# Turning the keys before the result, and longer gaps between copies and the products that use them, in a fused recurrence and expert kernel

## The chip, the cores and the metric

The kernel runs on one core of one Trainium2 chip. The metric is the device time of one execution in microseconds (us). The kernel before takes 1080.8 us (median of 4 runs, 1079.32 to 1081.3). All runs in this document are of the state "fast": none took over 1.5% longer than the fastest run of its kernel. A single core has no second die to be compared with, so the only sign of disturbance is the granted clock of TensorE (the share of its full speed at which it was let run, as the trace records it), which was recorded for each run and which matters here.

## The reference

Two blocks follow each other. The first is a gated linear recurrence over 768 positions for 4 batches and 8 heads of width 48. The second mixes 4 experts, each a two-layer network of width 1024, over the 3072 rows that the first block makes.

```python
for t in range(S):                                  # S = 768
    state = alpha[:, :, t, :, None] * state + einsum('bhd,bhe->bhde', k[:, :, t], v[:, :, t])
    y[:, :, t] = einsum('bhd,bhde->bhe', q[:, :, t], state)
x = y.transpose(0, 2, 1, 3).reshape(3072, 384)
p = domain_probs / (domain_probs.sum(-1, keepdims=True) + 1e-09)
for e in range(4):
    out += p[:, e:e + 1] * (relu(x @ w1[e]) @ w2[e])
```

## The kernel before

The recurrence is cut into 24 *units*, one for each chunk of 128 positions and each batch. A unit is a Python generator: every `yield` ends a step, and each step sends some instructions to several engines. The experts run in groups of up to four units (512 rows), and the steps of later units are dealt out between the expert matmuls of earlier ones. The program gives each engine one list of instructions, so a step's place decides how much other work lies between a copy on ScalarE and the product on TensorE that needs it.

The last steps of a unit, cut to what matters:

```python
        copy_q(6)                       # beat 11: ScalarE copies the last queries
        next_q(6)
        yield
        ...                             # beat 12: far = products across a chunk, then sc = levels 4 and 5
        yield
        parts = lat.rearrange("p (r s i) c -> p r s i c", s=2, i=2)
        ...                             # beat 13: ScalarE copies far to lat
        yield
        for s in range(2):              # beat 14: ScalarE copies near to lat
            rows = slice(HALF * s, HALF * (s + 1))
            nc.scalar.copy(out=lat[rows, :, rows], in_=near[rows])
        KT = KTs[-1]
        yield
        yps = ps.tile([P, KC, P], F32, name="yps", tag="w")
        ...                             # beat 15: the result, yps, from lat, v, QT and the state
        yield
        if cb < NCB - 1:
            KB = AT                     # beat 16: keys turned on TensorE, copied by ScalarE
            nc.scalar.copy(out=KB, in_=turned(lambda p: KT[:, p, :]))
            yield
            sps = ps.tile([P, NP, 2, D], F32, name="sps", tag="w")
            ...                         # beat 17: sps = keys x values, added to the state
```

And how steps get their place. `deal` computes for each unit an interval in the scheduler's own count of time, and `advance` sends the steps that have fallen due:

```python
    BEATS = 17
    ...
                events += [(begin + (end - begin) * (j + 1) / BEATS, u, run) for j in range(BEATS)]
    ...
    def advance(spent):
        nonlocal clock
        clock += spent
        while waiting and clock >= waiting[0][0]:
            next(waiting.popleft()[2], None)
```

Units 0 and 1 have their own hand-made order. Units 2 to 5 must be done during the first expert group, which is also when the weights are split into parts (ScalarE and VectorE) and stored for later (`kept`). Their intervals are less than half as long as those of later units.

## Time and profile before

| before, profiled run | value |
|---|---|
| span | 1079.8 us |
| TensorE busy | 1055.5 us (98%) |
| TensorE waits, total idle | 24.3 us |
| of it: yps behind lat, far behind queries | 8.4 us, 4.6 us |
| stretches at half clock before the end | 82.0 to 85.4 and 123.0 to 129.8 us |

The kernel is bound by TensorE, so only idle time and slow time on TensorE count. The view of waits names for each idle stretch what ended it. A window view gives busy time in a stretch together with the granted clock. Its columns are: stretch; length; busy us (instructions) of TensorE, of its weight loads, of VectorE, ScalarE and GpSimd; granted clock; DMA share; GB/s. For the kernel before, in the two stretches behind the long waits and one later on:

```profile
82.00:86.00 4.00, 4.00 (x60) 2.93 (x60) 3.96 (x8) 2.92 (x9) 0.53 (x1) 0.57 0.35 125
122.00:130.00 8.00, 5.64 (x54) 3.73 (x55) 4.33 (x11) 4.66 (x11) 0.53 (x1) 0.57 0.60 237
167.00:171.00 4.00, 4.00 (x45) 2.82 (x40) 3.93 (x9) 1.69 (x4) 1.06 (x2) 1.00 1.01 424
```

The granted clock is 0.57 in the first two: TensorE is nearly at half speed there. The share of busy time doesn't show this, since a slow matmul counts as busy.

### The profile page before, as it was taken

The page shows a single profiled execution, that of the slowest core. Times are in us where ns is not written, and L with a number is a line of the kernel's source. Part 1 is how long each engine was busy: PE and PEld are TensorE (multiplying, and loading weights), DVE is VectorE, ACT ScalarE, POOL GpSimd, SP SyncE. Part 2 cuts the span into 40 slices and gives each one's busy share as a digit, 9 for nine tenths or more (in the row PEclk, how much of TensorE's full clock was granted, in tenths as well). Part 3 has the DMA queues.
Part 4 walks back from the last instruction along what each step waited for, and adds up shares of the span by engine and source line. Part 5 has one row for each costly group of instructions (what it writes and reads, how often), then busy time and mean ns, then how long its engine had stood idle before and what let it go on. Part 6 is the DMA issues. An engine that isn't in the chain of part 4 may idle for free.

```text
span 1079.8 us, 21595 instructions
## 1 busy us (share of the span) xinstructions
PE 1055.5 (98%) x8460; PEld 899.6 (83%) x8460; DVE 774.5 (72%) x1711; ACT 566.8 (52%) x1202; POOL 32.7 (3%) x71
## 2 busy tenths in 40 slices
PE   8889899999999999999999999999999999999998
PEld 8767677676777798898898998888989889898988
DVE  5588678656557878777877786986878866666565
ACT  5786766764747455536446445555564543323232
POOL 2000000000000100000000000000000000000000
PEclk9999899999999999999999999999999999999999
DMA  8597679886686968659568568595594643544440
GB/s 124 155 329 227 213 230 378 301 315 240 234 295 208 399 203 318 253 147 351 204 221 324 195 228 320 159 327 222 168 352 146 249 191 136 215 172 180 182 182 33
DMA packets 158838, 251.67 MB, mean 233 GB/s; under 512 B 120112, under 2 KB 135344, under 8 KB 136208
## 3 DMA queue, kind: packets, MB, share of 16 engines
q1 hardware_dynamic: 149600, 208.82, 56.2%
q0 software_dynamic: 5760, 41.29, 9.7%
q8 instruction: 67, 1.10, 0.4%
q10 hardware_dynamic: 3376, 0.17, 0.3%
q14 instruction: 35, 0.29, 0.1%
HBM read 207.79 MB, written 42.47 MB: 232 GB/s over the span
## 4 chain that ended last, share of the span: by engine, by line
PE 80%; DVE 8%; ACT 6%; issue 2%; SPq 2%; DMA 1%; ACTq 0%; DVEq 0%
PE ops L615 26%; PE one L531 21%; PE two L531 10%; PE ops L619 9%; PE sc L333 5%; PE yps L425 3%; PE tp L265 2%; ACT qb L307 2%; PE one L523 2%; PE sps L454 1%; DVE near L343 1%; DVE hT L571 1%; PE far L388 1%; DVE t L544 1%; SPq L211 1%
## 5 line engine op out<-in xcount | busy, mean ns | idle before, releaser
L615 PE MATMUL ops<-w,hT 128*128 128x384 f32 x1728 | 318.6, 340 | 2.8 <-DVE acc L649 2.8
L615 PEld LDWEIGHTS ops<-w,hT 128*128 128x128 f32 x1728 | 299.1, 188 | 8.2 <-DVE acc L649 4.1
L531 PE MATMUL one<-xT,w 128*128 128x512 f32 x960 | 253.7, 400 | 0.8 <-DMA w<-kept 0.5
L531 PEld LDWEIGHTS one<-xT,w 128*128 128x128 f32 x960 | 175.9, 188 | 42.0 <-issue 2.4
L542 ACT ACTIVATE t<-one 128x512 f32<-128x512 f32 (+1 forms) x192 | 106.5, 555 | 163.8 <-PE one L531 144.1
L307 ACT COPY qb<-QT 64x256 f32<-64x256 f32 x336 | 136.5, 406 | 72.0 <-DVE QT L288 34.8
L569 ACT ACTIVATE hT<-t 128x512 fp32r<-128x512 f32 (+1 forms) x160 | 94.3, 589 | 111.3 <-DVE t L544 110.1
L571 DVE SCALAR_TENSOR_TENSOR hT<-t,hT 128x512 fp32r<-128x512 f32 (+1 forms) x160 | 102.0, 638 | 60.5 <-ACT hT L569 58.8
L531 PE MATMUL two<-xT,w 128*128 128x512 f32 x480 | 136.3, 392 | 0.0
L619 PE MATMUL ops<-hT 128*128 128x384 f32 x384 | 135.8, 497 | 0.0
L544 DVE TENSOR_TENSOR t<-t,two 128x512 f32<-128x512 f32 (+1 forms) x160 | 100.8, 630 | 39.5 <-ACT t L542 21.1
L581 DVE SCALAR_TENSOR_TENSOR hT<-hT 128x256 fp32r<-128x256 f32 x288 | 112.0, 421 | 4.4
L531 PEld LDWEIGHTS two<-xT,w 128*128 128x128 f32 x480 | 90.2, 188 | 19.8
L619 PEld LDWEIGHTS ops<-hT 128*128 128x128 f32 x384 | 70.0, 192 | 40.5 <-issue 1.4
L343 DVE COPY_PREDICATED near<-masks,sc 128x256 f32<-128x256 uint8 x144 | 77.0, 535 | 18.0 <-PE sc L333 14.9
L314 DVE TENSOR_TENSOR QT<-QT,dec 128x256 f32<-128x256 f32 x144 | 60.7, 421 | 34.3 <-ACT qb L307 33.9
L333 PEld LDWEIGHTS sc<-qb,KT 128*64 128x64 f32 x2304 | 73.3, 139 | 9.2 <-issue 7.1
L333 PE MATMUL sc<-qb,KT 128*64 128x64 f32 x2304 | 77.6, 224 | 0.2 <-ACT qb L307 0.2
L649 DVE SCALAR_TENSOR_TENSOR acc<-ops,p_all,acc 128x384 f32<-128x384 f32 x82 | 49.4, 612 | 29.1 <-PE ops L615 14.2
L326 DVE TENSOR_TENSOR KT<-KT,dec 128x256 f32<-128x256 f32 x144 | 60.2, 418 | 2.8 <-PE tp L265 2.8
L325 ACT COPY KT<-KT 128x256 f32<-128x256 f32 x144 | 59.7, 415 | 3.1
L549 DVE TENSOR_TENSOR hT<-t,two 128x512 f32<-128x512 f32 x32 | 22.0, 688 | 35.5 <-ACT t L542 28.6
(88 smaller groups left out, 972.6 us busy)
## 6 DMA issues: line engine op xcount, KB each, us to landing
w<-kept SPq DMA_DIRECT2D x144, 1152.0 KB
kept<-w POOLq DMA_DIRECT2D x32, 1152.0 KB, 7.6
hT<-in_moe_w_dram SPq DMA_DIRECT2D x32, 384.0 KB
w<-in_moe_w_dram SPq DMA_DIRECT2D x48, 128.0 KB
ra<-in_alpha_dram SPq DMA_DIRECT2D x23, 192.0 KB
rk<-in_k_dram SPq DMA_DIRECT2D x23, 192.0 KB
rq<-in_q_dram SPq DMA_DIRECT2D x23, 192.0 KB
out_dram<-acc POOLq DMA_DIRECT2D x18, 192.0 KB, 6.4
```

What stands on the lines that cost most here:

```text
L307: nc.scalar.copy(out=qb[rows, :, i, :].rearrange("p a (b r) -> p a b r", r=m), in_=qv[rows])
L314: nc.vector.tensor_mul(qv, qv, spread(dv[:, :, :, 0], m))
L333: nc.tensor.matmul(out[HALF * s:HALF * (s + 1), 2 * p:2 * p + 2, :], lhsT=KTs[li][:, p, HALF * s:HALF * (s + 1)], rhs=qbs[li][:, p, :, QUA ...
L343: nc.vector.copy_predicated(near.rearrange("p a (b two r) -> p a b two r", two=2, r=m)[:, :, :, 1, :], mk.unsqueeze(1).broadcast_to([P, H, ...
L531: nc.tensor.matmul(out, lhsT=w[:, part, kc], rhs=x_part(gi, part, kc), start=(part == terms[0] and kc == 0), stop=(part == terms[-1] and k ...
L542: nc.scalar.activation(out=t, in_=one, func=ACT.Copy, scale=FINE)
L544: nc.vector.tensor_add(t, t, two)
L569: nc.scalar.activation(out=top, in_=x, func=ACT.Relu, scale=TRIM)
L571: nc.vector.scalar_tensor_tensor(out=low, in0=x, scalar=0.0, in1=top.bitcast(F32), op0=ALU.max, op1=ALU.subtract)
L581: nc.vector.scalar_tensor_tensor(out=dif, in0=top.bitcast(F32), scalar=1 / 4096.0, in1=low.bitcast(F32), op0=ALU.mult, op1=ALU.subtract)
L615: nc.tensor.matmul(sums[i][part // 2], lhsT=h[:, part], rhs=w, start=(fc == 0 and part != 1), stop=(fc == FCH - 1 and part != 0))
L619: nc.tensor.matmul(sums[i][0], lhsT=h[:, 2].bitcast(F32), rhs=w, start=(fc == 0), stop=(fc == FCH - 1))
```

## The change

The intent is to give the copies on ScalarE more time before TensorE needs what they make. From unit 2 on the keys are turned before the result, and the beats are spaced unevenly. No instruction is added or removed. The diff, without the lines that are only indented anew:

```diff
-    BEATS = 17
+    BEATS = [*(0.055 * (j + 1) for j in range(11)), 0.69, 0.75, 0.8, 0.87, 0.94, 1.0]
...
-        yps = ps.tile([P, KC, P], F32, name="yps", tag="w")
+        def result():
+            yps = ps.tile([P, KC, P], F32, name="yps", tag="w")
             ...                      # the body as before
-        yield
+
+        def turn_keys():
+            if cb < NCB - 1:
+                nc.scalar.copy(out=AT, in_=turned(lambda p: KT[:, p, :]))
+
+        for step in (turn_keys, result) if u >= half else (result, turn_keys):
+            step()
+            yield
 
         if cb < NCB - 1:
             KB = AT
-            nc.scalar.copy(out=KB, in_=turned(lambda p: KT[:, p, :]))
-            yield
...
-                events += [(begin + (end - begin) * (j + 1) / BEATS, u, run) for j in range(BEATS)]
+                events += [(begin + (end - begin) * beat, u, run) for beat in BEATS]
```

More of the change, by code (lines that the diff above doesn't have):

```diff
@@ L411, in attention @@
         flat_v = rv.rearrange("p (a i) d -> p a (i d)", i=2)
-        yps = ps.tile([P, KC, P], F32, name="yps", tag="w")
-        for c in range(KC):
-            if c < 2:
-                now = [[(2 * c + j // 2, j % 2, (0, HD + TAIL)[j % 2], 2 * QUAD * (j % 2))
-                        for j in range(4)]]
-                turns = ([(True, now[0])] if cb > 0 else []) + [(False, now[0])]
-            else:
-                turns = [(True, [(p, 0, 0, QUAD) for p in range(NP)])] if cb > 0 else []
-                turns += [(False, [(p, i, QUAD + TAIL * i, 0) for p in range(NP)]) for i in range(2)]
-            for n, (past, turn) in enumerate(turns):
-                for j, (p, i, in_v, in_st) in enumerate(turn):
-                    nc.tensor.matmul(
-                        yps[QUAD * j:QUAD * (j + 1), c, :],
-                        lhsT=flat_st[:, p, in_st:in_st + QUAD] if past
-                        else flat_v[:, p, in_v:in_v + QUAD],
-                        rhs=QT[:, p, :] if past else lat[:, 2 * p + i, :],
-                        start=(n == 0), stop=(n == len(turns) - 1))
@@ L431, in attention @@
-        gi, slot = place[cb, b]
-        if slot == 0:
-            if gi == 0:
-                xTs[gi] = work.tile([P, 3, KC, NT], F32R, name="xT", bufs=1)
-                xraws[gi] = xTs[gi][:, 2].bitcast(F32)
-            elif gi < LAST:
-                xraws[gi] = work.tile([P, KC, NT], F32, name="x_raw", bufs=1)
-            else:
-                xraws[gi] = []
-        if gi < LAST:
-            nc.scalar.copy(out=xraws[gi][:, :, slot * P:(slot + 1) * P], in_=yps)
-        else:
-            xraws[gi].append(AT)
-            nc.scalar.copy(out=AT[:, :KC, :], in_=yps)
@@ L446, in attention @@
-        yield
+        def result():
+            yps = ps.tile([P, KC, P], F32, name="yps", tag="w")
+            for c in range(KC):
+                if c < 2:
+                    now = [[(2 * c + j // 2, j % 2, (0, HD + TAIL)[j % 2], 2 * QUAD * (j % 2))
+                            for j in range(4)]]
+                    turns = ([(True, now[0])] if cb > 0 else []) + [(False, now[0])]
+                else:
+                    turns = [(True, [(p, 0, 0, QUAD) for p in range(NP)])] if cb > 0 else []
+                    turns += [(False, [(p, i, QUAD + TAIL * i, 0) for p in range(NP)]) for i in range(2)]
+                for n, (past, turn) in enumerate(turns):
+                    for j, (p, i, in_v, in_st) in enumerate(turn):
+                        nc.tensor.matmul(
+                            yps[QUAD * j:QUAD * (j + 1), c, :],
+                            lhsT=flat_st[:, p, in_st:in_st + QUAD] if past
+                            else flat_v[:, p, in_v:in_v + QUAD],
+                            rhs=QT[:, p, :] if past else lat[:, 2 * p + i, :],
+                            start=(n == 0), stop=(n == len(turns) - 1))
+            gi, slot = place[cb, b]
+            if slot == 0:
+                if gi == 0:
+                    xTs[gi] = work.tile([P, 3, KC, NT], F32R, name="xT", bufs=1)
+                    xraws[gi] = xTs[gi][:, 2].bitcast(F32)
+                elif gi < LAST:
+                    xraws[gi] = work.tile([P, KC, NT], F32, name="x_raw", bufs=1)
+                else:
+                    xraws[gi] = []
+            if gi < LAST:
+                nc.scalar.copy(out=xraws[gi][:, :, slot * P:(slot + 1) * P], in_=yps)
+            else:
+                xraws[gi].append(AT)
+                nc.scalar.copy(out=AT[:, :KC, :], in_=yps)
```

## The prediction

> **What bounds the kernel now.** I read the busy table first, then what TensorE waits for over the whole span, then its timeline at the two longest of those waits.
>
> ```profile
> PE 1055.5 (98%) x8460; PEld 899.6 (83%) x8460; DVE 774.5 (72%) x1711; ACT 566.8 (52%) x1202; POOL 32.7 (3%) x71
> PEclk9999899999999999999999999999999999999999
> ```
>
> TensorE is bound: 1055.5 of 1079.8 us busy, so 24.3 us idle in all. The clock row has one slice, the fifth (108 to 135 us), visibly below the others. The waits of TensorE (us in total, times, longest):
>
> ```profile
> PE yps L425 <- ACT lat L405: 8.4, 5, 3.5
> PE far L388 <- ACT qb L307: 4.6, 4, 1.6
> PE ops L615 <- DVE acc L649: 2.8, 4, 1.2
> PE sps L454 <- ACT AT L450: 1.3, 1, 1.3
> ```
>
> The first, second and fourth rows are what the change aims at: the result (yps), the product across a chunk (far) and the state product (sps), each standing behind a ScalarE copy. But they are not spread over the 24 attention units. The same view by stretches puts 3.0 us of far, the whole 1.3 us of sps and 0.3 us of yps before 50 us, in units 0 and 1. Of the rest, yps loses 2.7 us (one wait) in 50 to 90 us, 4.5 us (two) in 90 to 180 and 0.9 us (one) in 700 to 860; far 1.2, 0.4 and 0.2. From 180 to 480 us TensorE shows no wait at all (199.97 of 200 and 100.00 of 100 us busy). So the change can pay only at a few places, nearly all in units 2 to 5, whose events the scheduler squeezes into the first expert group. TensorE's timeline there (start, us, what, idle before):
>
> ```profile
> 72.14 0.66 PE L388 MATMUL far<-qb,KT 128*64 128x128 f32 x8 [1.23 <-ACT qb L307]
> ...
> 80.54 1.08 PE L425 MATMUL yps<-lat,rv 128*32 128x128 f32 x32 [2.73 <-ACT lat L405]
> ```
> ```profile
> 120.44 0.42 PE L425 MATMUL yps<-QT,st 128*32 128x128 f32 x8
> 124.36 0.65 PE L425 MATMUL yps<-lat,rv 128*32 128x128 f32 x8 [3.50 <-ACT lat L405]
> 124.79 0.65 PE L425 MATMUL yps<-QT,st 128*32 128x128 f32 x8
> 125.22 0.65 PE L425 MATMUL yps<-lat,rv 128*32 128x128 f32 x8
> 125.64 0.65 PE L425 MATMUL yps<-QT,st 128*32 128x128 f32 x8
> 126.07 1.08 PE L425 MATMUL yps<-lat,rv 128*32 128x128 f32 x16
> 127.08 2.89 PE L619 MATMUL ops<-hT 128*128 128x384 f32 x4
> ```
>
> Two things are to be seen. The waits are 2.73 us (unit 2) and 3.50 us (unit 4); a third, of 0.97 us, stands at 100.56 us (unit 3). And after the second the work itself is slow: four ops matmuls take 2.89 us where four take 1.46 us at 143.20 us, and groups of eight yps that start 0.22 us apart in a later unit start 0.43 us apart. The trace's clock records have TensorE at 0.5 from 82.0 to 85.4 us and from 123.0 to 129.8 us, just behind these two waits and nowhere else before the end.
>
> **What the Trainium skill says.** "TensorE: Matmul & The Clock Gate", section "What's actually happening": the array clock falls to half after about one idle window of 3.4 us and comes back after a busy one; the windows run freely; the page's term for the cost is throttled time × (1 − K/N). This trace agrees: the low stretches last 3.4 and 6.8 us, one and two windows, and the pace halves. The waits of 1.58 us (far, at 40.60) and 1.23 us do not bring one. "Perfetto Trace Analysis", section "Optimization Strategy": look for gaps on the bound engine within the regime and ask which semaphore ends them; that is the reading above. Its "Summary: the profiler window per engine type" calls the end of a TensorE record an estimate, so I count in start times.
>
> **The change part by part.** No instruction is added or removed. (a) A unit's 17 beats were spaced by 1/17 = 0.059 of its interval. Now the first 11 are spaced by 0.055, and the copy of the last queries (beat 11) to far (beat 12) grows from 0.059 to 0.085. (b) From unit 2 on the keys are turned before the result. The near copy to lat (beat 14, now 0.80) stands 0.14 before the result (0.94) instead of 0.059; the copy of turned keys (0.87) 0.13 before sps (1.0). An interval in the first group is 23 of the scheduler's units, in which its 63.4 took about 125 us (47 to 172), so 0.059 is about 2.7 us there and 0.14 about 6.3. But events fall only at set places of the expert loop, so I read what moves from the order of both built programs.
>
> Unit 4, the 3.50 us wait. ScalarE before it:
>
> ```profile
> 121.60 0.38 ACT L525 ACTIVATE hT<-one 128x256 f32<-128x256 f32 x1
> 121.88 0.84 ACT L307 COPY qb<-QT 64x256 f32<-64x256 f32 x2
> 122.75 0.42 ACT L325 COPY KT<-KT 128x256 f32<-128x256 f32 x1
> 123.07 1.24 ACT L405 COPY lat<-near 64x512 f32<-64x512 f32 x2
> ```
>
> In the new order one pair of qb copies and one KT copy fewer stand ahead of the near copies (0.82 + 0.43 = 1.25 us), and on TensorE the result comes later by one transpose group (0.44) and two ops (1.30). 1.25 + 1.74 = 3.0, so some 0.5 us of 3.50 is left. Such a wait is too short to lower the clock: of 124.4 to 129.8 us, 5.4 us at half pace, 2.7 come back. Together 5.7 us.
>
> Unit 3: its result moves behind a transpose group, one ops and three 256-wide products, 0.44 + 0.65 + 1.29 = 2.4 us; the wait of 0.97 goes.
>
> Unit 2: the near copies stand ahead of one relu and one weight split (0.28 + 0.74 on ScalarE), so they end near 79.4 instead of 80.5; TensorE gets only the transpose (0.44) in between. About 1.2 us of 2.73 is left, 1.5 gained. Its low clock (3.4 us, worth 1.7) may stay or go: I count 1.0.
>
> Far in units 2, 4 and later: 1.2 + 0.4 + 0.2 = 1.8 us. Unit 2's four earlier products come 2 us sooner on TensorE, while their last queries are still released at 63.1 us by a VectorE chain full of weight splits: a new wait of about 1 us takes most of it. Net 0.8. The late yps wait (unit at 806 us): 0.85 gained.
>
> Fewer changes of kind. In the chain, first after an attention group and then without one:
>
> ```profile
> 317.37 1.67 PE yps L425 x56
> 319.04 1.58 PE one L531 x6
> 323.81 1.39 PE one L531 x6
> ```
>
> The six matmuls behind a group cost 0.2 us more. In the new order the result stands directly beside the next unit's products in 13 units, and separate attention groups from the second expert group on fall from 124 to 117: 7 × 0.2 = 1.4 us.
>
> New waits: with the result and the next unit's products adjacent, those products come sooner by the ops and expert matmuls that used to stand between. In unit 2 and 3 I find their fourth query copy near 83.4 us, 1.3 us after TensorE could use it. I charge 1.3 there and 0.5 for the rest.
>
> Sum: 5.7 + 1.0 + 1.5 + 1.0 + 0.8 + 0.85 + 1.4 − 1.8 = 10.4 us. Not all of it need reach the end. At 172.86 us TensorE waits 0.5 us for the first kept weights; the weight loads there wait in the queue for the stores of the split pieces (17.5 us in four waits), so the end of the first group is nearly tied to ScalarE, VectorE and DMA too. These start from TensorE's own progress, so I let most pass and take 1 us off: 9.4 us, or 1071.5 us.
>
> **Rivals.** *Nothing gained:* the early part is bound by ScalarE and VectorE, and a removed wait comes back at the next operand. For: ScalarE and VectorE are busy 23.2 and 21.6 of 28 us from 47 to 75 us, and the weight chain at 172 us is nearly late. Against: ScalarE sits idle for 3.54 us before 89.94 and VectorE 1.24 before 88.25, both waiting for TensorE, so there is slack to hand on. It would make 1077 to 1081. *All gained:* yps 8.05, far 1.8, clock 4.4, changes of kind 1.4, no new waits, would be 15.7 us: 1065. Against it are the copies that demonstrably stay late in unit 2. *Worse:* the result lands 0.06 of an interval nearer the split of x that starts the next expert group, and the denser beats crowd VectorE so that the accumulations that free PSUM come later (the 2.8 us row doubles). For: 1.18 us are lost at 516.69 to just that. Against: the last result still stands some scheduler units before the end of the expert, and VectorE has over a quarter of its time free after 180 us. It would make about 1083.
>
> **Range and chances.** The three large terms, unit 4, unit 2 and the clock, decide: without the clock 1075, with everything 1065. 80% range 1066 to 1078. 2% would be 1059.2 us, beyond every removable wait, so faster 0.03; within 2% 0.95; slower 0.02.
>
> **What would show it.** In the changed kernel's waits: yps behind lat at 1.5 to 3 us instead of 8.4, far still near 3 to 4, sps and early far unchanged, a new row of sc behind ScalarE's queries of 1 to 3 us. No half clock near 115 to 125 us. From 180 us to the end the duration is the same within 3 us, the difference lies before. Wrong would be: gain after 180 us above 4 us (then changes of kind cost more than I read), a half clock still there, or a wait for kept weights of several us near 165 us that swallows the gain.

## The result, and the profile after

The changed kernel takes 1074.84 us (median of 4 runs, 1073.32 to 1075.73), the kernel before 1080.8. The ratio is 0.9946 with a 95% interval of 0.9928 to 0.9963, so the change is a small but real gain, within 2%. Ratios here are the mean time of one kernel's fast runs over the mean of the other's in the same rounds, so they are not quite the ratio of the medians. With 6 more runs of the changed kernel beside 19 of the kernel before, the ratio was 0.994 (0.9928 to 0.9952).

The lines of the page after the change that answer to those of before, busy time and clock:

```profile
PE 1048.1 (98%) x8460; PEld 899.1 (84%) x8460; DVE 775.2 (72%) x1711; ACT 566.7 (53%) x1202; POOL 32.7 (3%) x71
PEclk9999999999999999999999999999999999999999
```

TensorE's busy time is 7.4 us less with the same 8460 matmuls. That is one sign of a gain that is not waiting: the dip in the fifth slice of the clock row is gone. (The row is coarse: a slice is 27 us, and the single new stretch of 3.4 us shown below doesn't change its digit.) The waits of TensorE over the whole span (line numbers are 1 to 9 higher than before):

```profile
PE ops L624 <- DVE acc L658: 4.3, 4, 1.9
PE far L389 <- ACT qb L308: 3.1, 3, 1.6
PE yps L428 <- ACT lat L406: 3.1, 4, 1.5
PE sc L334 <- ACT qb L308: 2.6, 3, 1.2
...
PE one L540 <- DVE xT L248: 1.1, 1, 1.1
PE one L540 <- DVE QT L315: 1.0, 1, 1.0
```

The result's wait fell from 8.4 to 3.1 us, and far's from 4.6 to 3.1, of which 3.0 belong to units 0 and 1. But three rows have come or grown: the next unit's products behind the queries (sc, 2.6 instead of 0.2 us), the first matmuls of the second expert group (2.1 us instead of 0.7), and the products behind the accumulations (4.3 instead of 2.8). TensorE's timeline at units 2 and 4 shows the exchange:

```profile
80.25 1.08 PE L428 MATMUL yps<-lat,rv 128*32 128x128 f32 x32 [1.17 <-ACT lat L406]
81.26 1.65 PE L334 MATMUL sc<-qb,KT 128*64 128x64 f32 x48
84.12 0.69 PE L334 MATMUL sc<-qb,KT 128*64 128x64 f32 x16 [1.21 <-ACT qb L308]
...
121.38 0.43 PE L428 MATMUL yps<-lat,rv 128*32 128x128 f32 x8 [1.45 <-ACT lat L406]
```

Unit 2's result waits 1.17 us instead of 2.73, and the products that now follow it at once wait 1.21 us for their fourth copy of queries. Unit 4's result waits 1.45 us instead of 3.50. The same windows as before:

```profile
82.00:86.00 4.00, 2.79 (x52) 2.18 (x47) 3.76 (x9) 2.93 (x9) 0.50 (x1) 1.00 0.32 113
122.00:130.00 8.00, 8.00 (x123) 6.09 (x112) 7.46 (x22) 7.30 (x17) 0.53 (x1) 1.00 0.58 221
167.00:171.00 4.00, 3.78 (x12) 3.00 (x13) 1.87 (x4) 1.69 (x4) 0.54 (x1) 0.57 1.01 426
```

Both old half clock stretches are gone: TensorE does 123 matmuls from 122 to 130 us, where it did 54. In their place stands one new stretch at 167.4 to 170.8 us. It lies behind the first matmuls of the second expert group:

```profile
165.38 0.70 PE L540 MATMUL one<-xT,w 128*128 128x512 f32 x2 [0.99 <-DVE QT L315]
167.22 1.92 PE L540 MATMUL one<-xT,w 128*128 128x512 f32 x4 [1.13 <-DVE xT L248]
168.93 1.48 PE L540 MATMUL two<-xT,w 128*128 128x512 f32 x3
```

Two waits with 0.7 us of work between them, then matmuls at half pace (three products of kind two take 1.48 us here and 0.85 us at 172.34). The second wait is for the split of x on VectorE. The first is put down to VectorE here, but to the kept weights (0.9 us) in the profile of the repeated run, so the weights may be what it is.

Where the 8.2 us between the two profiled spans (1079.8 and 1071.6) lie can be read from the start of the same expert matmul, counted from 0 at the beginning, in both traces:

| expert matmul | before, us | after, us | after ahead by |
|---|---|---|---|
| 300th | 149.50 | 140.28 | 9.2 |
| 360th, some 3 us before the second group | 169.65 | 161.64 | 8.0 |
| 420th, in the second group | 187.95 | 182.54 | 5.4 |
| 4020th, near the end | 1065.46 | 1057.31 | 8.2 |

So 8 us were gained in the first expert group, 2.6 given back at its boundary, and 2.8 gained after it. Whether that last part is real is one of the questions for the experiments. The pair of profiles flatters the change by some 2 us: the profiled run of the kernel before took 1081.52 us, more than any of its four timed runs, at a granted clock of 0.995, where the mean of the 59 runs below is 0.997.

### The profile page after: what moved, and what is told of

It reads as the page before. It is cut to its first block, busy times and chain, and to the rows that moved or that the text cites. A ratio compares the mean times of both kernels' runs of the same rounds, so it can differ in the third digit from the quotient of the medians.

```text
span 1071.6 us, 21614 instructions
## 1 busy us (share of the span) xinstructions
PE 1048.1 (98%) x8460; PEld 899.1 (84%) x8460; DVE 775.2 (72%) x1711; ACT 566.7 (53%) x1202; POOL 32.7 (3%) x71
## 4 chain that ended last, share of the span: by engine, by line
PE 83%; DVE 8%; ACT 6%; issue 2%; DMA 1%; SPq 0%; DVEq 0%; ACTq 0%
PE ops L624 25%; PE one L540 21%; PE ops L628 10%; PE two L540 10%; PE sc L334 6%; PE yps L428 3%; PE tp L266 3%; PE one L532 2%; ACT qb L308 2%; PE far L389 1%; PE sps L463 1%; DVE near L344 1%; DVE t L553 1%; DVE hT L580 1%; DVE hT L590 1%
## 5 line engine op out<-in xcount | busy, mean ns | idle before, releaser
L628 PE MATMUL ops<-hT 128*128 128x384 f32 x384 | 133.4, 491 | 0.0
```

Source lines behind the costliest of these rows:

```text
L628: nc.tensor.matmul(sums[i][0], lhsT=h[:, 2].bitcast(F32), rhs=w, start=(fc == 0), stop=(fc == FCH - 1))
```

## The experiments

The theory: the gain lies in units 2 to 5 and consists of shorter waits and of the half clock behind them; part is given back at the boundary of the first expert group. Rivals: it comes from all 24 units (fewer changes between kinds of matmul), or from the beats, or the half clock costs nothing. All kernels gave a right result. Each ran in 5 rounds beside the kernel before. There were three calls, on three chips, and each shared 19 to 21 runs of it: the first four experiments in one, then e4 to e7 (only units 6 on, the half clock, the earlier split, the 8 products), then the control and the combinations. Across calls the ratios are to be compared and not the times.

**The change again.** No edit.

> The changed kernel again, to tighten its ratio and to stand beside the others on the same chip. Expected 0.994 to 0.995 of before (1074 to 1075 us).

1073.72 us (1072.05 to 1076.65), ratio 0.994 (0.9928 to 0.9952). Its spread has a pattern: the run with a granted clock of 1.0 spans 1070.3 us, four with 0.998 span 1071.9 to 1072.1, the one with 0.996 spans 1074.9. One half clock stretch of 3.4 us is 0.5 × 3.4 / 1072 = 0.0016 of the mean clock, and 1.7 us of time. So the runs most likely differ by how many such stretches they have. Not all spread is clock: three runs of the next kernel at a clock of 1.0 span 1069.9 to 1072.0 us.

**Only the order.**

```diff
-    BEATS = [*(0.055 * (j + 1) for j in range(11)), 0.69, 0.75, 0.8, 0.87, 0.94, 1.0]
+    BEATS = [(j + 1) / 17 for j in range(17)]
```

> Only the new order of steps (keys turned ahead of the result), with the old even beats. Theory (waits of units 2 to 5 and the half clock behind them are the gain): unit 4's result stands behind a transpose and two ops more, so about 1.7 us of its 3.5 us wait is left and its half clock (2.7 us) goes; unit 3's 0.97 us goes; unit 2 keeps some 2.3 us and its half clock. Some 6 us gained before the second expert group, 1 to 3 us given back there: ratio 0.995 to 0.997. Rival (the gain comes from the beats and from results standing directly beside the next unit's products, which this kernel has in 2 units only): no gain, ratio 0.998 to 1.000.

1073.78 us, ratio 0.9933 (0.992 to 0.9946): all of the gain, and more than I had put down to it. Its waits:

```profile
PE yps L428 <- ACT lat L406: 2.3, 1, 2.3
PE far L389 <- ACT qb L308: 1.2, 1, 1.2
PE sc L334 <- ACT qb L308: 0.2, 1, 0.2
```

These are from 50 to 90 us. Unit 2 waits 2.3 us for its result, as expected, and far still waits 1.2, while sc waits only 0.2. From 90 to 180 us the result waits 1.8 us and far 0.4. Together that is 5.9 us for the operands of attention; in the repeated run of the whole change it is also 5.9 (sc 2.6, yps 1.2 and 1.4, transposes 0.7). At the boundary this kernel waits 2.3 us in one piece for the kept weights. This profile is of the slowest of its five runs (1076.56 us) and shows half clock behind unit 2's result (81.2 to 84.6 us) and at the boundary (170.0 to 173.4 us). Three of the five runs have a granted clock of 1.0, so in them unit 2 did not keep its half clock, against the expectation, which is where the gain exceeds it.

**Only the beats.**

```diff
-        for step in (turn_keys, result) if u >= half else (result, turn_keys):
+        for step in (result, turn_keys):
```

> Only the new beats, with the old order (result ahead of the keys). Theory: near copies stand 1.25 us earlier in ScalarE's queue but TensorE comes to the result no later; unit 4 keeps about 2.2 us and unit 2 about 1.6 us of wait, and a half clock behind unit 4 may stay. Ratio 0.996 to 0.999, less gain than with the order alone. Rival (beats are the main part): ratio near 0.995, as with the whole change.

1080.26 us (13 runs), ratio 0.9997 (0.9989 to 1.0006): nothing. In its profile unit 4 still waits 3.2 us and a half clock stretch stands behind it (123.5 to 127.0 us); sc has its new waits of 1.9 us. From 50 to 180 us the operands of attention cost 8.3 us of waits, where they cost 9.0 in the kernel before, and the boundary costs 2.2 instead of 0.7. So the beats alone move waits from one place to another and take hardly any away. The rival that they are the main part has fallen.

**Only units 2 to 5, and only units 6 on.** The condition `u >= half` becomes the one shown, and other units use even beats and the old order.

```diff
+    EVEN = [(j + 1) / 17 for j in range(17)]
...
-        for step in (turn_keys, result) if u >= half else (result, turn_keys):
+        for step in (turn_keys, result) if 2 <= u < 6 else (result, turn_keys):
...
-                events += [(begin + (end - begin) * beat, u, run) for beat in BEATS]
+                events += [(begin + (end - begin) * beat, u, run)
+                           for beat in (BEATS if 2 <= u < 6 else EVEN)]
```

> The whole change for units 2 to 5 only, units 6 on as before. Theory: the gain of about 8 us before the second expert group stays, and what the later stages gave (2.8 us in the profiled pair) goes; if the give-back at the group's boundary (2.1 us of waits for VectorE and half a clock window) comes from unit 6's denser beats on VectorE, it goes too. Ratio 0.994 to 0.997. Rival (gain spread over all units): ratio 0.998 or more.

1074.15 us, ratio 0.995 (0.9934 to 0.9965). The gain of the first group is there. The boundary wait did not go with unit 6's beats: its profiled run, the longest of its six, waits 3.2 us there for the kept weights and has 6.8 us of half clock behind it. The wait for VectorE did go (0 instead of 1.1 us), as the expectation had it; a longer one for the kept weights stands in its place, so the total didn't fall. The table under the control below comes back to this.

The other half has `u >= 6` in both places.

> The whole change for units 6 on only, units 2 to 5 as before. Theory (the gain lies in units 2 to 5): only the late wait of 0.9 us and the fewer changes of kind (1.4 us by estimate) are gained, and the accumulations' waits may take part of it back: ratio 0.997 to 1.000, with the two half clock stretches of before still there. Rival (gain spread over all units): ratio 0.996 or less.

1080.68 us (14 runs), ratio 1.0008 (0.9998 to 1.0019): no gain from the 18 later units, and the rival of a gain spread over all units has fallen. In its profile the late wait of 0.9 us for lat is gone, but this has come:

```profile
770.19 3.79 PE L625 MATMUL ops<-w,hT 128*128 128x384 f32 x12 [1.91 <-DVE acc L659]
```

A wait of 1.91 us for an accumulation on VectorE, and the twelve matmuls behind it take 3.79 us; in the repeated run of the whole change the same twelve take 2.35 us after the same wait. The records show a half clock from 770.7 to 774.1 us here and none there. The mean granted clock of its 14 runs is 0.995, against 0.997 in 59 runs of the kernel before. Yet the later units do gain something in the traces. From the 420th to the 4020th expert matmul this profile takes 877.4 us, of which the half clock is 1.7; the four kernels whose later units are as before take 877.0 to 877.5, and the five profiles of kernels with the whole change 874.8 to 875.9. So some 2 us are gained there, and in this kernel's time they are lost again: its boundary waits 2.1 us instead of 0.7, and the lower clock costs some 2 us more, differently from run to run.

**The half clock by itself.** In the kernel before, TensorE is kept busy during the two long waits, with products of the identity into the part of the result's buffer that real products overwrite later. The copies that it waits for are untouched.

```diff
         yps = ps.tile([P, KC, P], F32, name="yps", tag="w")
+        for _ in range({2: 11, 4: 14}.get(u, 0)):
+            nc.tensor.matmul(yps[:, 2, :], lhsT=ident, rhs=ident, start=True, stop=True)
```

> The kernel before, with TensorE kept at work during the two waits: 11 products of the identity into the still unused result buffer of unit 2 and 14 in unit 4, some 2.3 and 3.0 us. The copies that end the waits are untouched. Theory (the half clock behind the waits is a cost of its own, 1.7 and 2.7 us by the trace): both stretches vanish, ratio 0.996 to 0.998, granted clock 0.999 or 1.0 in most runs. Rival (the half clock costs nothing, since other engines bound that stretch): ratio 0.999 to 1.001.

1076.95 us (8 runs, 1076.67 to 1077.26), ratio 0.9972 (0.9962 to 0.9982), granted clock 0.999 or 1.0 in all 8. TensorE at unit 4:

```profile
119.01 3.29 PE L414 MATMUL yps<-ident 128*128 128x128 f32 x28
122.22 0.43 PE L427 MATMUL yps<-QT,st 128*32 128x128 f32 x8
123.08 0.42 PE L427 MATMUL yps<-lat,rv 128*32 128x128 f32 x8 [0.43 <-ACT lat L405]
...
124.53 1.56 PE L621 MATMUL ops<-hT 128*128 128x384 f32 x4
```

The 14 products show as 28 records. The result starts no sooner than the copies allow, but the four ops matmuls behind it take 1.56 us where they took 2.89. Useless work made the kernel 3 us faster, because the half clock behind a wait was a cost of its own. The rival that it costs nothing has fallen. The 8 runs also vary by only 0.6 us, where the 21 of the kernel before vary by 5.0 (1077.29 to 1082.28 in that call). The kernel itself already sends such products at its start, between the steps of units 0 and 1 (`idle`, never read).

**The boundary.** In the changed kernel the later three steps of splitting x for the second expert group are issued earlier.

```diff
-                    for step, at in enumerate((0.0, 0.52, 0.62, 0.72)):
+                    for step, at in enumerate((0.0, 0.3, 0.4, 0.5) if after[0] == 1
+                                              else (0.0, 0.52, 0.62, 0.72)):
```

> The changed kernel with the three later steps of the split of x for the second expert group issued earlier (at 0.3, 0.4, 0.5 instead of 0.52, 0.62, 0.72 of the last expert). Theory (VectorE gives back gain at the group's boundary): the wait of 1.1 us for VectorE there goes, the wait of 1 us for kept weights may stay or grow; 1 to 3 us less than the changed kernel, ratio 0.991 to 0.993. Rival (the kept weights' own chain bounds the boundary): as the changed kernel, 0.994.

1071.56 us (6 runs, 1070.55 to 1072.45), ratio 0.9924 (0.9909 to 0.9938), the lowest of all kernels here, though its interval overlaps those of several others. In its profile one wait is left at the boundary and no half clock:

```profile
165.96 1.63 PE L540 MATMUL one<-xT,w 128*128 128x512 f32 x6 [1.48 <-DVE KT L327]
```

The name of the releaser can't be taken at its word: that VectorE instruction writes keys that this matmul doesn't read, and the last split of x that it does read started at 163.37 us and took 0.69. What is left is most likely the kept weights. The intervals of this kernel and of the unaltered change overlap a little (0.9909 to 0.9938 against 0.9928 to 0.9952), and the two ran on different chips, so the gain of some 1.7 us is likely and not certain. In the profiles it is plain: from the 360th to the 420th expert matmul it takes 18.4 us, the change 20.9 and the kernel before 18.3.

**Keeping the clock up at the boundary.** The changed kernel, with 8 products of the identity at the boundary instead of the earlier split.

```diff
         one = ps.tile([P, NT], F32, name="one", tag="g", bufs=4)[:, :hi - lo]
+        for _ in range(8 if (gi, e, fc) == (1, 0, 0) else 0):
+            nc.tensor.matmul(one[:, :P], lhsT=ident, rhs=ident, start=True, stop=True)
```

> The changed kernel with 8 products of the identity (1.7 us) ahead of the second expert group's first matmul, into a buffer which that matmul starts afresh. Theory (the half clock behind the boundary's waits costs up to 1.7 us in the runs that have it): granted clock 1.0 in nearly all runs, less spread, ratio 0.992 to 0.993. Rival (the products only stand in the way): ratio 0.994 to 0.996.

1072.48 us (6 runs, 1071.65 to 1073.55), ratio 0.9931 (0.9918 to 0.9944). The direction and the smaller spread are as expected, but the interval overlaps that of the change, and two of six runs still have a granted clock of 0.998. It supports the half clock at the boundary as a cost of about a microsecond, no more.

**Control: the earlier split in the kernel before.** The same edit to the kernel before.

> The kernel before with the earlier split steps alone, as control for the changed kernel with them (0.9924). Theory (the boundary holds back only a kernel that gets there sooner; before waits 0.7 us there and has no half clock there): ratio 0.999 to 1.000. Rival (the earlier split is worth its 2 us by itself, so the boundary had nothing to do with the lost gain): ratio 0.997 to 0.998.

1079.33 us (14 runs), ratio 0.9993 (0.9984 to 1.0002): nothing clear. This alone would fit a boundary that holds back only a kernel that comes to it sooner, but two kernels that were no faster, only the beats and only units 6 on, also wait 2.1 to 2.2 us there. The profiles tell two causes apart. "Ready" is the start of the second group's first matmul less its wait; the split of x ends with a step on VectorE that the same matmuls need.

| kernel | beats of unit 6 | TensorE ready, us | last step starts, us | later by | wait for weights, for x |
|---|---|---|---|---|---|
| before | even | 172.39 | 173.08 | 0.7 | 0.5, 0.3 |
| only the order | even | 166.36 | 167.04 | 0.7 | 2.3, 0 |
| only units 2 to 5 | even | 164.84 | 165.26 | 0.4 | 3.2, 0 |
| only units 6 on | new | 171.22 | 173.30 | 2.1 | 0.2, 1.9 |
| only the beats | new | 169.40 | 171.50 | 2.1 | 0.5, 1.7 |
| the change again | new | 164.46 | 166.56 | 2.1 | 0.9, 1.2 |

With the new beats, 2.6 us of attention's work stands on VectorE between the last two steps of the split, without them 1.1 us. So the wait for x comes from unit 6's new beats, whenever TensorE arrives. The wait for the kept weights is the one that grows the sooner TensorE comes, within each kind of beats. The earlier split takes away the first, which the kernel before hardly has; that most likely is why it helps the change alone.

**Combinations.** The earlier split and the 8 products, on the whole change:

> The changed kernel with the earlier split steps and the 8 products that keep the clock at the boundary. If both act on the same wait they do not add: ratio 0.992. If they are independent: 0.991.

1072.43 us, ratio 0.9928 (0.9915 to 0.9941): they don't add. The new order with even beats and the earlier split:

> The new order with the old even beats and the earlier split steps. Theory (the beats bring nothing net, since what they take from result and far they add at the next unit's products): as the changed kernel with the earlier split, ratio 0.991 to 0.993. Rival (the beats are needed): 0.994 or more.

1073.87 us, ratio 0.9942 (0.9929 to 0.9956). The earlier split did not help the order alone (0.9933), which has even beats and no wait for x. Its profile waits 0.6 us for kept weights at the boundary instead of 2.3, then 0.6 us for expert weights (hT) at 189.9 us, and keeps unit 2's half clock (80.9 to 84.3 us), with none at the boundary. Whether the beats are worth something once the split is early (0.9924 against 0.9942) is not settled: the intervals overlap. The same kernel with products of the identity in all the waits that are left, at the boundary as above and in units 2 and 4:

```diff
+            for _ in range({2: 9, 4: 7}.get(u, 0)):
+                nc.tensor.matmul(yps[:, 2, :], lhsT=ident, rhs=ident, start=True, stop=True)
```

> The kernel before this one with TensorE kept at work in the waits that are left: 9 products ahead of unit 2's result, 7 ahead of unit 4's, 8 at the boundary. Theory: granted clock 1.0 in nearly every run, some 1 to 2 us less than without, ratio 0.990 to 0.991, the fastest of all. Rival (fills delay as much as the clock costs): no change.

1073.94 us, ratio 0.9944 (0.993 to 0.9959). The granted clock was 1.0 in five of six runs and 0.999 in the sixth, as expected, but the time didn't fall. In its profile 1.4 us are waited for expert weights by DMA behind the boundary, up to 189.91 us, the same moment at which the profile without the fills stops waiting for them. So in this pair of profiles a transfer took back what the fills gave; that it is so in the other runs isn't shown. This expectation was a miss.

## Why the prediction was right or wrong

The total was right: 1071.5 us predicted with 1066 to 1078, 1074.84 measured (1073.72 in the repeat). The gain was over-estimated: 9.4 us against 6.0 (6.8 in the repeat, by medians). By its own steps:

- **The gain lies in units 2 to 5.** Right for the time. Those units alone give 0.995, the later ones 1.0008.
- **Unit 4: 0.5 us left of 3.5, and no half clock.** The half clock went; the wait that is left is 1.45 us. TensorE reached the expert matmuls ahead of the result 2.67 us sooner (114.34 instead of 117.01), since unit 2 and 3 had been gained, but the near copies ended only 3.0 us sooner (121.3 instead of 124.3). Of the 1.25 us that ScalarE's queue was to save, some 0.3 was left: the pair of qb copies and the KT copy no longer stand behind the weight split but stand ahead of it, and ScalarE could start them only at 115.60 us, after 1.42 us of waiting for VectorE.
- **Unit 3's 0.97 us goes, unit 2's wait falls to about 1.2 us, new waits of 1 and 1.3 us at the next units' products, far gone in units 2 and 4.** All as predicted: 0, 1.17, 1.20 and 1.21 us, and no far wait from 50 to 180 us.
- **The half clock gives 2.7 + 1.0 us.** Right in kind, and near in size where it was looked for: removing it alone gives 3 us (0.9972). But it counts by the run, and the size was read from one run with more of it than most: 58 of 59 fast runs of the kernel before had a clock below 1.0, but their mean is 0.997, that of the profiled run 0.995, some 2 us apart.
- **Fewer changes of kind give 1.4 us, the late wait 0.85.** In the traces both are there, and the first was put too low. The separate attention groups did fall from 124 to 117, and TensorE's busy time from the 420th to the 4020th expert matmul is 869.6 to 870.9 us in the five profiles with the whole change and 872.8 to 873.7 in the seven with 124 groups: some 3 to 4 us. That the groups are the cause is likely and not tested by itself. New waits for accumulations (4.3 instead of 2.8 us) leave a net gain of 2.8 us in the profiled pair. As a gain in time of the later units alone it doesn't show (1.0008), since the boundary and the clock take it back. The prediction had accumulations, and beats that crowd VectorE ahead of the split of x, only in its third rival.
- **"I let most pass and take 1 us off."** This is the term that was most clearly mis-sized. At the boundary the waits grew from 0.7 to 2.1 us and a half clock stretch worth up to 1.7 us came: 2.6 us by the profile (8.0 us ahead at the 360th expert matmul, 5.4 at the 420th). The prediction looked only at the kept weights; more than half of the new waiting is for the split of x, behind unit 6's new beats on VectorE. The experiments point the same way: the earlier split gives 0.9924 instead of 0.994 (some 1.7 us), while it gives the kernel before nothing.
- **The beats.** The prediction added their part to that of the order. Alone they bring nothing, in part because they delay the split of x at the boundary, and the order alone brings everything. What they took from unit 2's result and far they added at the products that followed. With all these waits counted, both kernels stood 5.9 us behind attention's operands from 50 to 180 us.

An estimate of the split: span times mean granted clock is what a run would have spanned at full clock, if all time at half clock were matmul time. It gives 1074.9 us for the 59 runs of the kernel before and 1070.1 for the repeat of the change. So some 4.8 us of the gain are waits and order. Of the 6.1 us between the mean spans (1078.3 and 1072.2) the remaining 1.3 are clock, where 3.7 had been predicted, because the boundary brings a new stretch and because the mean run of the kernel before had less half clock to lose than the profiled one. That the total fell inside the range owes something to luck: the part for the later units was too small, and those for the boundary and the clock erred the other way. Not settled: what exactly releases the first kept weights, and what the beats are worth when the split is early.

## What to carry to other kernels

When TensorE is 98% busy, look for the few places where it waits, and then behind each of them for a stretch of low clock: here those stretches cost about 3 us, half as much as the two waits of 6.2 us that caused them, and busy time hid it. Moving a step to put other work between a copy and its use helps if that work would have been done anyway; spreading the steps in time, by itself, moved the wait to the next operand, and it put 1.5 us more of other work ahead of the split that starts the next stage. A gain in one stage arrives early at the next one's transfers, so look there for what is given back, and check on each engine what a moved step now stands in front of.

## What the Trainium skill lacked or had wrong

- "TensorE: Matmul & The Clock Gate" puts the fall to half clock after an idle window of about 3.4 us (section "What's actually happening") and advises against idle gaps above about 3 us (section "Why this matters for your kernels"). Here one wait of 2.73 us (unit 2), two waits of 0.99 and 1.13 us with 0.7 us of work between them, and in one run a wait of 1.91 us were followed by a half clock stretch, while the same wait of 1.91 us was not in another run.
- The same page says that the windows run freely and that the number of slow matmuls at a kernel's start varies from run to run for that reason. It has no figure for stretches later on: here runs of one kernel on one chip differ by some 1.7 us for each stretch (spans of 1070.3, 1072 and 1074.9 us at a granted clock of 1.0, 0.998 and 0.996), so small changes need the clock of every run beside its time.
- No page that I read has the remedy measured here: matmuls without use into a buffer that is overwritten later, during a known wait, made the kernel before 3 us faster (0.9972) and cut its spread from 5.0 to 0.6 us. It did not help the kernel with the new order, even beats and the earlier split (0.9944 with, 0.9942 without).
